# Storing a transform's first rows ahead of the rest, and a maximum negated per sign: one change to a fused FFT and gated MLP kernel

## The chip, the cores and the metric

One core of one Trainium2 chip. The metric is device time in microseconds (us) for one launch. The kernels were timed in rounds beside runs of the kernel before on the same chip. Single runs of one kernel differ (the kernel before: 1200.54 to 1205.46), so parts of a few us are read from the trace, and totals from several rounds.

The traces name the engines of the core: PE multiplies matrices, DVE does vector work, ACT functions and copies, POOL small sums and some transfers, SP issues most transfers. SBUF is the memory on the chip, DRAM the one beside it.

## The reference

```python
X = np.fft.fft(np.fft.fft(x, axis=1), axis=2).real      # x: (8, 3136, 256)
h = X.reshape(25088, 256) @ w_in                        # d_ff = 1024
e = np.exp(h - h.max(-1)); sm = e / (e.sum(-1) + 1e-9)
u = h * sm
ln = (u - mean(u)) / sqrt(var(u) + 1e-6) * g_ln
out = ln @ w_out                                        # back to 256
```

The weights come as 64-bit floats and are converted on the chip by integer operations.

## The kernel before

The sequence of 3136 is split as 49 x 64. Two batches form a pair. For each pair a first transform of length 49 runs in eight pieces c, called quarters in these texts (`transform1`, 98 rows in, 100 rows out: 25 frequencies k1 with 4 parts j each). Its result z goes to DRAM (`zd`), and comes back turned (`turn`: 5 frequencies at a time) for the second transform. Then 25 units per pair follow, one for each k1: up-products, maximum, exponential, product, square, transposition, and, four units later, the down-product. A unit has two signs (k1 and its mirror), but k1 = 0 has one. For pairs 1 to 3 the transform runs beside the units of the pair before. For pair 0 nothing hides it: this start is what the change is about.

```python
def transform1(pr, s):                       # cut
    c, l = divmod(2 * s, CH)
    if l == 0:
        if pr.p == 0 and c % 2:              # two buffers z_u and two buffers z
            z = fpool.tile([P, FF], FP32, tag="u", name="z_u", bufs=2)
            pr.z = z[0:ZR].rearrange("p (l d) -> p l d", l=CH)
        else:
            pr.z = zpool.tile([ZR, CH, D], FP32, tag="z", name="z")
    ...                                      # matmuls into ps
    nc.scalar.copy(pr.z[:, l : l + 2, :], ps[0:ZR])
    if l == CH - 2:
        nc.sync.dma_start(out=pr.zd[:, c * CH : (c + 1) * CH, :], in_=pr.z)   # ZR = 100 rows

def turn(pr, i):
    pr.g[i] = gpool.tile([P, KG, D], FP32, tag="g", name="g")                 # six buffers
    for j in range(4):
        k = j * NK + i * KG
        nc.gpsimd.dma_start(out=pr.g[i][j * NH : (j + 1) * NH, :, :],
                            in_=pr.zd[k : k + KG, :, :].rearrange("k n d -> n k d"))

# join(): both maxima, then one negation of both; expo(): exponential of each sign
nc.scalar.mul(out=t.neg[:, 0:n], in_=t.nmax[:, 0:n], mul=-1.0)

# the start
for c in range(NC):                          # cut
    add_mirror(first, c, nc.vector); fold(first, c)
    ...                                      # c == 3: load raw_out, the output weights
    for s in range(CH // 2): transform1(first, c * CH // 2 + s)
turn(first, 0)
...
for i in range(KF * D // NW): weights.narrow_out(i)      # DVE converts raw_out to Wo: 4 times
for t in units[:2]: take2(t, transform2(pairs[0], t.k1)); spread(t)           # spread loads r
# unit: even() = L223 needs r, Wi, w_mid; unit 0 also centres Wo (L457 to L459)
```

Of the kernel before, what the change touches and what calls it, by code (L numbers as in the profile page):

```python
# [9 lines left out]
FP32 = mybir.dt.float32  # L10
# [6 lines left out]
P = 128  # L17


N1, N2 = 49, 64  # L20
NK = N1 // 2 + 1
# [3 lines left out]
CH = 4  # L25
# [9 lines left out]
def kernel(  # L35
# [57 lines left out]
    class Pair:  # L93
        def __init__(self, p):
            self.p = p
            self.raw, self.y, self.y0 = {}, {}, None
            self.g = {}

    def load(pr, c, room=None):

# [42 lines left out]
    def transform1(pr, s):  # L143



        c, l = divmod(2 * s, CH)
        if s == 0:
            pr.zd = dram.tile([ZR, NH, D], FP32, tag="zd", name="zd")
        if l == 0:  # L150
            if pr.p == 0 and c % 2:

                z = fpool.tile([P, FF], FP32, tag="u", name="z_u", bufs=2)
                pr.z = z[0:ZR].rearrange("p (l d) -> p l d", l=CH)
            else:
                pr.z = zpool.tile([ZR, CH, D], FP32, tag="z", name="z")
        y = pr.y[c]
        ps = ps_m.tile([P, 2, D], FP32, tag="m", name="ps1")
        if s == NH // 2 - 1:
            parts = [(ps[0:ZR, 0], y[:, l], 0), (ps[0:ZR, 1], pr.y0[:, 0], 1), (ps[0:ZR, 1], y[:, l + 1], 2)]  # L160
        else:
            parts = [(ps[0:ZR], y[:, l : l + 2], 0)]
        first = True
        for o, i, t in parts:
            for h, cs in enumerate((EVEN, ODD)):
                nc.tensor.matmul(o[..., cs], F[:, 2 * t + h, :], i[..., cs], start=first, stop=True,  # L166
                                 skip_group_check=True)
                first = False
        nc.scalar.copy(pr.z[:, l : l + 2, :], ps[0:ZR])
        if l == CH - 2:  # L170
            nc.sync.dma_start(out=pr.zd[:, c * CH : (c + 1) * CH, :], in_=pr.z)

    def turn(pr, i):

        pr.g[i] = gpool.tile([P, KG, D], FP32, tag="g", name="g")
        for j in range(4):
            k = j * NK + i * KG
            nc.gpsimd.dma_start(out=pr.g[i][j * NH : (j + 1) * NH, :, :],  # L178
                                in_=pr.zd[k : k + KG, :, :].rearrange("k n d -> n k d"))

    def transform2(pr, k1):

# [43 lines left out]
    def join(t, ps):  # L226

        t.nmax = small.tile([P, 2], FP32, tag="nmax", name="nmax")
        for s in t.signs:
            t.h[s] = fpool.tile([P, FF], FP32, tag="h", name="h", bufs=2)  # L230
            nc.vector.tensor_tensor_reduce(out=t.h[s], in0=t.ev, in1=ps, scale=1.0, scalar=-3.0e38,  # L231
                                           op0=ALU.subtract if s else ALU.add, op1=ALU.max,
                                           accum_out=t.nmax[:, s : s + 1])
        n = len(t.signs)
        t.neg = small.tile([P, 2], FP32, tag="neg", name="neg")
        nc.scalar.mul(out=t.neg[:, 0:n], in_=t.nmax[:, 0:n], mul=-1.0)  # L236

    def expo(t):
        t.esum = small.tile([P, 2], FP32, tag="esum", name="esum")
        for s in t.signs:  # L240
            t.u[s] = fpool.tile([P, FF], FP32, tag="u", name="u", bufs=2)
            nc.scalar.activation(out=t.u[s], in_=t.h[s], func=ACT.Exp, bias=t.neg[:, s : s + 1],  # L242
                                 accum_out=t.esum[:, s : s + 1])
# [71 lines left out]
    def down(t, s):  # L315
        uT = t.batch.uT[:, t.w].rearrange("p c i (n s) -> p c (i n) s", s=2)
        ps = ps_m.tile([P, D], FP32, tag="m", name="ps_o")
        for c in range(KF):
            nc.tensor.matmul(ps, uT[:, c, :, s], Wo[:, c, :], start=(c == 0), stop=(c == KF - 1))  # L319
        return ps  # L320

    def scale(t, s, ps):
        t.ot[s] = fpool.tile([P, D], FP32, tag="ot", name="ot", bufs=6)
        nc.scalar.mul(out=t.ot[s], in_=ps, mul=t.rs[:, s : s + 1])  # L324
# [165 lines left out]
    with tc.manual_schedule():  # L490
# [25 lines left out]
        for c in range(NC):  # L516
# [16 lines left out]
                transform1(first, c * CH // 2 + s)  # L533
            if c == 3:
                weights.product_in(0)
        turn(first, 0)
        weights.place_table()
        for h in range(1, 3):
            weights.product_in(h)
# [9 lines left out]
        for i in range(len(units) + lag):  # L549
            cur = units[i] if i < len(units) else None  # L550
            nxt = units[i + 2] if i + 2 < len(units) else None
            old = units[i - lag] if i >= lag else None
            ahd = pairs[cur.p + 1] if cur and cur.p + 1 < NP else None
            last = i >= len(units) - 2
            prv = units[i - 1] if 0 < i <= whole else None
            if i > lag:
                store(units[i - lag - 1])
            if cur:
                if i % 2 == 0:
                    batch = Batch(i >= whole)  # L560
                cur.batch, cur.w = batch, i % 2
                even(cur, up(cur, 0))
                odd = up(cur, 1)
            if nxt:
                take2(nxt, transform2(pairs[nxt.p], nxt.k1))
                spread(nxt)
            if prv:
                turn_whole(prv)
            if cur:
                join(cur, odd)  # L570
            if prv:
                for o, ps in prv.wait:
                    nc.vector.tensor_copy(out=o, in_=ps)
            if cur:
                expo(cur)
            if ahd:
                ahead_pe(ahd, cur.k1)
            if old:
                ps_o = [down(old, s) for s in old.signs]
            if cur:  # L580
                for s in cur.signs:
                    product(cur, s)
                if i == 0:
                    weights.centre()
                for s in cur.signs:
                    square(cur, s)
                    if i >= whole:
                        turn_blocks(cur, s)
            if old:
                scale(old, 0, ps_o[0])  # L590
            if cur:
                if last:
                    move_blocks(batch, slice(cur.w, cur.w + 1), (nc.sync, nc.gpsimd) if cur.w else (nc.sync,))
                elif cur.w and i >= whole:
                    move_blocks(batch, slice(0, 2))
                stats(cur)
            if 0 < i + 1 < NK // KG:
                turn(first, i + 1)
            if ahd:
                ahead(ahd, cur.k1)  # L600
            if old and 1 in old.signs:
                scale(old, 1, ps_o[1])
        store(units[-1])


def _tables(B, S, D):

    import numpy as np

    def cs(num, den):  # L610
        a = 2.0 * math.pi * (num % den) / den
        return np.cos(a), np.sin(a)

    n1, k1 = np.arange(N1)[:, None], np.arange(NK)[None, :]
    c, s = cs(n1 * k1, N1)
    cm, sm = cs((n1 - N1 // 2) * k1, N1)
    zero = np.zeros_like(c)
    tabs = [(c, s), (s, -c), (c, zero), (s, zero), (zero, cm), (zero, sm)]
    f = np.zeros((2, N1, 6, 2, 2, NK))
    for t, (u, v) in enumerate(tabs):  # L620
        for b in range(2):
            f[b, :, t, b, 0], f[b, :, t, b, 1] = u, v
    k = (np.arange(NK)[:, None] + N1 * np.arange(N2)[None, :])[None]
    n2 = (np.arange(NH) + 1) % NH
    c, s = cs(n2[:, None, None] * k, S)
    t = np.stack([c, -s])
    t[1, -1] = 1.0 - 2.0 * (k[0] % 2)
    m, d = np.arange(D)[:, None], np.arange(D)[None, :]
    q = np.where(d <= D // 2, cs(m * d, D)[0], -cs(m * (d - D // 2), D)[1])

    q = np.concatenate([q, q[:, D // 2 : D // 2 + 1]], axis=1)
    q[:, D // 2] = 0.0
    sign = np.where(np.arange(P) == 0, 1.0, -1.0)[:, None]
    row = np.arange(B)[:, None] * N1 + np.arange(N1)[::-1]

    load = row.reshape(-1, PR, 1) * (N2 // CH) + N2 // CH - 1 - np.arange(NC)
    mirror = np.zeros((P, B // 2 * (NC + NK - 1)), np.int32)
    mirror[:PR, : B // 2 * NC] = load.transpose(1, 0, 2).reshape(PR, -1)
    rows = np.arange(B)[:, None, None] * S + (N1 - np.arange(1, NK)) + N1 * np.arange(N2)[::-1, None]
    mirror[:, B // 2 * NC :] = rows.reshape(B // 2, P, NK - 1).transpose(1, 0, 2).reshape(P, -1)  # L640
    return {
        "f_tab": f.reshape(PR, 6, ZR).astype(np.float32),
        "t_tab": t.reshape(2 * NH, NK, N2).astype(np.float32),
        "q_tab": q.astype(np.float32),
        "sign": sign.astype(np.float32),
        "mirror": mirror,
    }
# [32 lines left out]
```

## Time and profile before

| | before |
|---|---|
| time, median of the first 3 runs | 1204.17 us (1202.84 to 1204.25) |
| profiled span, mean granted clock | 1200.8 us, 0.993 |
| busy: PE, DVE, ACT, POOL | 96%, 75%, 53%, 45% |
| second transform of unit 0 starts | 68.25 us |
| first vector step of unit 0 (L223) | 73.04 us |
| first down-product (L319) | 107.65 us |
| last scaling on ACT, end of the span | 1196.01, 1200.8 us |

PE is the engine in short supply from 110 us on, so time can be won only before that or after its last product. In the page's part 2 the span is cut into 40 slices of 30 us; a digit is the busy share in tenths. Of the kernel before:

```profile
PE   2868999999999999999999999999999999999998
DVE  8778877777768877777767887877777787777770
```

Only the first four digits of PE and the last are low, and in the first four DVE is busy there. The prediction shows these slices in detail.

### The profile page before, as it was taken

To read this page: it belongs to the slowest core of one execution; us is meant where nothing else is said; L and a number is where in the kernel's file an instruction comes from. 1 tells how busy PE (TensorE), PEld (TensorE's weight loads), DVE (VectorE), ACT (ScalarE), POOL (GpSimd) and SP (SyncE) were. 2 spreads that over 40 slices of the span, in tenths; PEclk is the share of its full clock that TensorE was granted. 3 is DMA by queue.
4 is the path that set the end of the run, shared out by engine and by line. 5 is a ranking of instruction groups with operands and counts; after the bars stand their busy time and mean duration, and the time that the engine had idled before them with its cause. 6 is when DMAs were issued, how large, how long until landed. Compare 5 with 4: busy or idle time off the path is not lost. (4 is left out here: it accounts for less than half of the span.)

```text
span 1200.8 us, 15804 instructions
## 1 busy us (share of the span) xinstructions
PE 1155.5 (96%) x4720; PEld 877.0 (73%) x4720; DVE 905.8 (75%) x1255; ACT 640.4 (53%) x1286; POOL 543.8 (45%) x966
## 2 busy tenths in 40 slices
PE   2868999999999999999999999999999999999998
PEld 1446777777777777777777777777877777777787
DVE  8778877777768877777767887877777787777770
ACT  1337555655555655655554665655554555555551
POOL 3046545554645555443554555444453333333333
PEclk9989999999999999999999999999999999999999
DMA  9833799978999798777999799797899586776765
GB/s 237 257 92 82 142 174 162 192 134 158 184 162 170 167 177 164 175 132 140 169 178 189 144 185 166 159 168 137 160 171 159 94 139 115 134 129 109 132 111 114
DMA packets 457382, 184.98 MB, mean 154 GB/s; under 512 B 425510, under 2 KB 439086, under 8 KB 457296
## 3 DMA queue, kind: packets, MB, share of 16 engines
q1 hardware_dynamic: 443216, 144.89, 68.5%
q0 software_dynamic: 14080, 39.08, 12.4%
q8 instruction: 38, 0.62, 0.2%
q14 instruction: 48, 0.39, 0.1%
HBM read 44.37 MB, written 38.80 MB: 69 GB/s over the span
## 5 line engine op out<-in xcount | busy, mean ns | idle before, releaser
L319 PE MATMUL ps_o<-Wo,uT 128*128 128x256 f32 x3136 | 693.4, 379 | 0.0
L319 PEld LDWEIGHTS ps_o<-Wo,uT 128*128 128x128 f32 x3136 | 611.6, 196 | 61.8 <-issue 1.0
L217 PE MATMUL ps_h<-Wi,q 128*128 128x512 f32 x800 | 362.5, 596 | 0.1
L250 DVE SCALAR_TENSOR_TENSOR u<-h,u 128x1024 f32<-128x1024 f32 x196 | 232.6, 1223 | 153.5 <-ACT u L242 95.7
L259 ACT ACTIVATE h<-u,nmean 128x1024 f32<-128x1024 f32 x196 | 223.7, 1142 | 123.4 <-POOL nmean L252 123.3
L252 POOL TENSOR_SCALAR nmean<-usum 128x1 f32<-128x1 f32 x196 | 127.0, 649 | 348.4 <-DVE u L250 348.1
L231 DVE CUSTOM_DVE_ANT_0 h<-ev,ps_h 128x1024 f32<-128x1024 f32 x196 | 231.8, 1219 | 44.6 <-PE ps_h L217 38.4
L217 PEld LDWEIGHTS ps_h<-Wi,q 128*128 128x128 f32 x800 | 152.7, 191 | 150.0 <-issue 143.9
L287 DVE STREAM_TRANSPOSE v<-u 128x1024 f32<-128x1024 f32 x192 | 228.2, 1230 | 0.1
L242 ACT ACTIVATE u<-h,neg 128x1024 f32<-128x1024 f32 x196 | 223.6, 1142 | 3.3
L223 DVE SCALAR_TENSOR_TENSOR ev<-w_mid,r,ps_h 128x1024 f32<-128x1024 f32 x100 | 127.7, 1277 | 55.0 <-PE ps_h L217 49.8
L195 ACT COPY q<-ps 128x256 f32<-128x256 f32 x100 | 37.2, 372 | 183.0 <-PE ps L189 155.5
L331 POOL DMA_INDIRECT out_dram<-ot,idx x96 | 102.8, 1071 | 33.3 <-issue 18.4
L236 ACT ACTIVATE neg<-nmax 128x2 f32<-128x2 f32 (+1 forms) x100 | 20.4, 204 | 175.2 <-DVE nmax L231 140.8
L189 PEld LDWEIGHTS ps<-T,g 128*128 128x128 f32 x400 | 60.9, 194 | 59.0 <-issue 56.8
L271 POOL TENSOR_SCALAR v<-ssq 128x2 f32<-128x2 f32 (+1 forms) x100 | 27.6, 276 | 167.2 <-ACT h L259 167.2
L166 PE MATMUL ps<-y,F 98*100 98x258 f32 (+3 forms) x288 | 72.7, 390 | 24.6 <-DVE y L122 23.8
L324 ACT ACTIVATE ot<-ps_o,rs 128x256 f32<-128x256 f32 x196 | 83.3, 459 | 24.0 <-DMA out_dram<-ot,idx 12.8
L274 POOL TENSOR_TENSOR rs<-v,neg_half 128x2 f32<-128x2 f32 (+1 forms) x100 | 72.5, 725 | 7.8
L166 PEld LDWEIGHTS ps<-y,F 98*100 98x100 f32 x288 | 46.3, 179 | 37.0 <-DVE y L122 21.3
L189 PE MATMUL ps<-T,g 128*128 128x128 f32 x400 | 61.6, 278 | 11.3 <-DMA g<-zd 11.3
L178 POOL DMA_DIRECT2D g<-zd x80 | 47.8, 607 | 47.2 <-DMA zd<-z_u 38.7
(68 smaller groups left out, 465.0 us busy)
## 6 DMA issues: line engine op xcount, KB each, us to landing
uT<-v SPq DMA_DIRECT2D x752, 128.0 KB
g<-zd POOLq DMA_DIRECT2D x80, 160.0 KB, 4.8
out_dram<-ot SPq DMA_DIRECT2D x100, 128.0 KB
zd<-z SPq DMA_DIRECT2D x28, 400.0 KB
xa<-in_x_dram SPq DMA_DIRECT2D x28, 392.0 KB
raw_in<-in_moe_w_in_dram SPq DMA_DIRECT2D x4, 512.0 KB
raw_out<-in_moe_w_out_dram SPq DMA_DIRECT2D x2, 1024.0 KB
zd<-z_u SPq DMA_DIRECT2D x4, 400.0 KB
```

The lines of the kernel that those rows point to most:

```text
L166: nc.tensor.matmul(o[..., cs], F[:, 2 * t + h, :], i[..., cs], start=first, stop=True, skip_group_check=True)
L189: nc.tensor.matmul(ps[:, h * P : (h + 1) * P], g[:, k, h * P : (h + 1) * P], T[:, k1, :], start=(h == 0), stop=True, skip_group_check=True)
L217: nc.tensor.matmul(ps[:, fs], t.q[:, c * P : (c + 1) * P], Wi[:, c, fs], start=True, stop=True)
L223: nc.vector.scalar_tensor_tensor(out=t.ev, in0=w_mid, scalar=t.r, in1=ps, op0=ALU.mult, op1=ALU.add)
L231: nc.vector.tensor_tensor_reduce(out=t.h[s], in0=t.ev, in1=ps, scale=1.0, scalar=-3.0e38, op0=ALU.subtract if s else ALU.add, op1=ALU.max, ...
L242: nc.scalar.activation(out=t.u[s], in_=t.h[s], func=ACT.Exp, bias=t.neg[:, s : s + 1], accum_out=t.esum[:, s : s + 1])
L250: nc.vector.scalar_tensor_tensor(out=t.u[s], in0=t.h[s], scalar=1.0, in1=t.u[s], op0=ALU.mult, op1=ALU.mult, accum_out=t.usum[:, s : s + 1])
L252: nc.gpsimd.tensor_scalar(out=t.nmean[:, s : s + 1], in0=t.usum[:, s : s + 1], scalar1=-1.0 / FF, scalar2=None, op0=ALU.mult)
L259: nc.scalar.activation(out=t.h[s], in_=t.u[s], func=ACT.Square, bias=t.nmean[:, s : s + 1], accum_out=t.ssq[:, s : s + 1])
L287: nc.vector.transpose(out=t.batch.v[:, t.w, :, o], in_=t.u[s])
L319: nc.tensor.matmul(ps, uT[:, c, :, s], Wo[:, c, :], start=(c == 0), stop=(c == KF - 1))
L331: dma = nc.gpsimd.indirect_dma_start(out=out, out_offset=bass.IndirectOffsetOnAxis(ap=idx[:, i : i + 1], axis=0), in_=t.ot[s], in_offset=None)
```

## The change

The intent: the second transform needs, for its first five frequencies, only 20 of the 100 rows of each quarter. So rows are laid out frequency first, 20 rows of each quarter are stored at once, the first turn is issued on two queues, and only then do the other 80 rows follow, from buffers kept for it (four of the six g buffers, which are free at that time). Beside it, the maxima are negated by sign, and the last unit's two signs swap places so that the last store is a direct one (the other sign's rows are stored indirectly, through a table of row numbers).

```diff
-            if pr.p == 0 and c % 2:
+            if pr.p or c < 2:
+                pr.z = zpool.tile([ZR, CH, D], FP32, tag="z", name="z")
+            elif c < 4:
                 z = fpool.tile([P, FF], FP32, tag="u", name="z_u", bufs=2)
                 pr.z = z[0:ZR].rearrange("p (l d) -> p l d", l=CH)
             else:
-                pr.z = zpool.tile([ZR, CH, D], FP32, tag="z", name="z")
+                pr.z = gpool.tile([P, KG, D], FP32, tag="g", name="z_g")[0:ZR, 0:CH, :]
+            pr.zs[c] = pr.z
@@
-            nc.sync.dma_start(out=pr.zd[:, c * CH : (c + 1) * CH, :], in_=pr.z)
+            keep(pr, c, slice(0, ZR if pr.p else 4 * KG))
+    def keep(pr, c, rows):
+        nc.sync.dma_start(out=pr.zd[rows, c * CH : (c + 1) * CH, :], in_=pr.zs[c][rows])
@@ turn: rows as (k j), engines[j] in place of nc.gpsimd
@@
-        t.neg = small.tile([P, 2], FP32, tag="neg", name="neg")
-        nc.scalar.mul(out=t.neg[:, 0:n], in_=t.nmax[:, 0:n], mul=-1.0)
@@ expo, in its loop over the signs
+            nc.scalar.mul(out=t.neg[:, s : s + 1], in_=t.nmax[:, s : s + 1], mul=-1.0)
@@
-        turn(first, 0)
+        turn(first, 0, (nc.sync, nc.gpsimd) * 2)
+        for c in (2, 3, 0, 1, 4, 5, 6, 7):
+            keep(first, c, slice(4 * KG, ZR))
@@
-                ps_o = [down(old, s) for s in old.signs]
+                order = old.signs[::-1] if old is units[-1] else old.signs
+                ps_o = [down(old, s) for s in order]
@@ scale() and the table of the first transform follow the new orders
```

## The prediction

> **What bounds the kernel now.** The page gives PE 96% of the span at a granted clock of 0.993, so I asked where the other 4% lies. The table of busy time by stretch (columns: stretch, its length, busy us with instruction counts of PE, PEld, DVE, ACT, POOL, then PE clock, DMA share, GB/s) answers:
>
> ```profile
> core 0: us, PE busy (x) PEld busy (x) DVE busy (x) ACT busy (x) POOL busy (x), PEclk, DMA share, GB/s
> 40.00:50.00 10.00, 9.21 (x45) 6.42 (x44) 6.45 (x16) 4.24 (x7) 0.00 (x0) 1.00 0.93 276
> 50.00:60.00 10.00, 6.95 (x17) 2.77 (x15) 8.45 (x18) 3.79 (x4) 0.00 (x0) 1.00 0.64 245
> 60.00:70.00 10.00, 1.75 (x8) 1.78 (x9) 9.04 (x19) 2.52 (x4) 2.48 (x4) 0.59 0.28 82
> 70.00:80.00 10.00, 10.00 (x34) 6.28 (x33) 4.72 (x6) 3.48 (x7) 1.11 (x2) 0.90 0.26 67
> 110.00:120.00 10.00, 10.00 (x42) 7.53 (x41) 8.28 (x12) 5.78 (x12) 5.92 (x10) 1.00 0.27 68
> ```
>
> From about 110 us PE is 10.00 of 10 in every stretch up to 1190. There each unit costs PE about 11 us of matmuls, and nothing in this stage leaves PE waiting. So any time won must be won before 110 us, or after PE's last matmul. A hole stands at 57 to 68 us, PE nearly idle. The table of waits for the first 70 us (waiter, awaited, us in total, times, longest) names it:
>
> ```profile
> POOL g L178 <- DMA zd<-z_u: 38.7, 1, 38.7
> PE ps L189 <- DMA g<-zd: 11.3, 1, 11.3
> ACT z_u L169 <- DMA zd<-z_u: 9.6, 2, 6.6
> DVE tmp L357 <- DMA raw_out<-in_moe_w_out_dram: 3.5, 1, 3.5
> ```
>
> The second transform (L189) waits for the turned buffer g, this for the last store of the first transform, this for its copy on ACT, and that one for an earlier store of the same buffer z_u. The timeline (start, us, engine, what, count) shows the same chain and, beside it, DVE:
>
> ```profile
> 47.41 0.16 DVE L122 COPY y<-x 98x2 f32<-98x2 f32 x1
> 51.10 0.43 DVE L357 TENSOR_SCALAR tmp<-raw_out 128x512 int32<-128x512 int32 x1 [3.53 <-DMA raw_out<-in_moe_w_out_dram]
> 56.20 1.07 ACT L169 COPY z_u<-ps 100x512 f32<-100x512 f32 x2 [6.57 <-DMA zd<-z_u]
> 57.29 0.27 SPq L171 DMA_DIRECT2D zd<-z_u  x1
> 63.02 2.48 POOL L178 DMA_DIRECT2D g<-zd  x4 [38.74 <-DMA zd<-z_u]
> 68.25 2.05 PE L189 MATMUL ps<-T,g 128*128 128x128 f32 x8 [11.30 <-DMA g<-zd]
> 68.64 0.88 DVE L380 SCALAR_TENSOR_TENSOR Wo<-raw_out,g_ln,tmp 128x256 f32<-128x256 f32 x2
> ...
> 73.04 1.28 DVE L223 SCALAR_TENSOR_TENSOR ev<-w_mid,r,ps_h 128x1024 f32<-128x1024 f32 x1 [3.52 <-PE ps_h L217]
> ...
> 79.02 2.29 DVE L459 TENSOR_TENSOR Wo<-Wo,wbar 128x2048 f32<-128x2048 f32 x1 [0.31 <-ACT wbar L458]
> ...
> 81.23 1.27 DVE L223 SCALAR_TENSOR_TENSOR ev<-w_mid,r,ps_h 128x1024 f32<-128x1024 f32 x1
> ...
> 85.29 1.15 ACT L242 ACTIVATE u<-h,neg 128x1024 f32<-128x1024 f32 x1
> ```
>
> The point to see is that two chains end together. PE starts at 68.25, but DVE converts the output weights (L357 to L380) from 51.10 to 69.52 and then waits only 3.52 us for PE. A first turn ten us earlier cannot be worth ten us unless DVE also finishes sooner.
>
> **What the Trainium skill says.** "DMA: Bandwidth & Descriptors", section "Why a DMA increments its semaphore by 16 and not by 1", says that a hardware-queue transfer runs on the largest number of engines, up to 16, that divides the slowest dimension of both sides, and names 100 partitions as 10. The trace agrees: while only stores of 100 rows are left (50 to 60 us) the DMA share is 0.64, near 10 of 16. By it the new 20-row stores have 10 engines, the 80-row ones 16.
> The same page, "Queues, rings and completion order", says that each engine consumes one queue's descriptors in ring order and alternates between queues by packets. So a tiny later load on SP's queue waits behind earlier stores; no number before shows that alone, and the change makes it matter. "Anatomy of one DMA" puts the fixed cost near 2.0 us for the software path; the lone first load here (idx, hardware queue) was issued at 0.74 and released POOL at 2.94, 2.2 us.
> "TensorE: Matmul & The Clock Gate", Part 1, says that the clock halves after an idle window of about 3.4 us and needs about as long to return. Agrees: last matmul 56.95, clock 0.50 from 62, work again at 68.25, clock 0.97 in 72 to 73.
>
> **The change, part by part.**
> (1) Bytes. Eight stores of 400 KB before the first turn become eight of 80 KB; 8 x 320 KB = 2.6 MB move behind it. Of this, stores 1 to 3 (28.72 to 35.78) lie ahead of the weight load raw_out (issued 38.33) in SP's queue: 0.98 MB less on 10 engines at 245 GB/s, 4 us. raw_out lands near 47 instead of 51. DVE's folds end at 47.57, before and after (they wait only 1.43 and 1.10 us, for things the change does not touch). So DVE starts converting at 47.6, not 51.1, and ends at 47.6 + 18.4 = 66.0, not 69.5: **3.5 us**.
> (2) Buffers. The last four quarters take g buffers, so ACT no longer waits 6.57 us. PE ends the first transform at 50.1; copies end near 50.7; the last store is issued near 50.8 instead of 57.29 and, with the queue almost empty, lands about 2.5 us later: 53.5. The turn is issued from two queues, 1.2 us instead of 2.48, and lands 2.7 us after its end (68.2 less 65.5 before): 57.5 to 58.5. PE is then free (product ends at 56.95). The second transform starts near **58, ten us earlier**; both halves of the first unit's up-product are ready by 63.
> (3) The late stores. 2.6 MB and part of the turn's 0.66 MB go ahead of the load of r, which L223 also needs. At 330 to 390 GB/s (the table shows 331 and 387 where all 16 engines work) 3.3 MB take 8 to 10 us from 54.5: drained at 63 to 64.5, r lands near 65 to 66. That is about when DVE comes free, so I count no cost but see the largest risk here.
> (4) So L223 for unit 0 starts at about 66.0 instead of 73.04: **7.0 us**, 3.5 from DVE and 3.5 from its wait for PE.
> (5) The column-sum product of the weights (16 matmul records, 3.6 us before) must wait for DVE's 66.0. PE will have idled 3 us or more, so probably part of it runs at half clock: ready at 70 (warm) to 71.5. L459 then starts at 71.4 to 72.3 against 79.02, a gain of 7.6 to 6.7; I take **6.7**, thus minus 0.3 on (4).
> (6) Negation by sign: 96 more ACT instructions of 204 ns, 20 us spread over ACT's 53%: hidden. In unit 1 the exponential of the first sign needs no longer wait for the second maximum: nmax at 83.87, ACT's copies done at 84.07, exponential at 85.29; it could start at 84.3: **1.0 us**. In units 2 to 4 the loop is exponential, product, mean, square, copies to uT, negation: 7.69 us a unit (88.86, 96.55, 104.24). ACT is still copying to uT until 92.73 when both maxima are nearly there (92.70), so nothing more is won.
> (7) The end. The last unit's sign order is reversed, so its last store is a direct one.
>
> ```profile
> 1196.01 0.47 ACT L324 ACTIVATE ot<-ps_o,rs 128x256 f32<-128x256 f32 x1 [2.98 <-PE ps_o L319]
> 1196.76 0.97 POOL L331 DMA_INDIRECT out_dram<-ot,idx  x1 [5.43 <-ACT ot L324]
> ```
>
> Now the indirect store takes 4.0 us from 1196.76 to the span's end at 1200.8. The direct one could be issued at 1196.5 and lands some 2.5 us later, 1199.0; the indirect one then starts 3.4 us earlier and ends first: **1.7 us**.
> (8) The interleaved row order changes addresses, not packets (1 KB) or bytes: 0.
> Sum: 6.7 + 1.0 + 1.7 = 9.4 us. I take 0.4 off for r or raw_out coming a little late: 9.0, hence 1195.2 us.
>
> **The rivals.**
> A: r comes late, the wait for g replaced by a wait for r. For it: the ring order and SP's long issue times under load (15.62 us once). If the late stores drain at 250 GB/s, 13 us from 54.5, r lands near 69: 4 us gained at (4), about 1199. Against: 80 rows spread over 16 engines.
> B: DVE does not move, because raw_out still waits for earlier x loads. Then only the 3.5 us wait for PE goes: total near 6, 1198. For it: DMA share is 0.93 to 1.00 up to 50 us.
> C: PE stays bound and the extra ACT work or the late stores' traffic slow the steady stage, so nothing is gained: 1204. Against: PE there has no waits for ACT worth naming and the late stores end before 70.
> D: better than thought: clock stays up and r is early: 8.6 + 1.7, 1193.5; with folds shortened too, 1191.
>
> **Range and chances.** Centre 1195.2, A and B give the upper side, D the lower: 1191 to 1199.5. Two per cent is 24 us, more than the whole hole before 68 us could give, since DVE's chain holds: faster 0.02, same 0.97, slower 0.01.
>
> **What will show it.** Right: first L189 near 58; first conversion of raw_out near 47.6 without a wait; first L223 near 66 with neither PE nor r as a long releaser; unit 1's exponential about 7.7 us earlier; PE full from about 100 us; the chain that ended last is a direct store. Wrong: L223 idle on r, conversion still waiting on raw_out, or a longer mean of the down-product L319 (379 ns) in the steady stage.

## The result

The changed kernel takes 1195.16 us (median of 6 runs, 1194.22 to 1200.61), the kernel before 1203.78 (6 runs): 8.6 us less. The ratio is 0.9938, 95% interval 0.9916 to 0.9960; a ratio is the mean time of one kernel's runs over that of the other's of the same rounds, so not quite the ratio of the medians. A second series (e11 below) gave 1195.89 against 1203.71, ratio 0.9939.

The lines of the changed kernel that answer to those in the prediction. First the waits of the first 70 us (lines have moved: L357 is L361, L223 is L228, L189 is L194):

```profile
POOL g L184 <- DMA zd<-z_g: 28.7, 1, 28.7
PE ps L194 <- DMA g<-zd: 3.7, 1, 3.7
DVE ev L228 <- DMA r<-q: 0.5, 1, 0.5
```

The wait of ACT for a z buffer (9.6 us) and that of DVE for raw_out (3.5 us) are gone, PE's wait for g fell from 11.3 to 3.7 us, and a new wait of 0.5 us for r has come. The timeline:

```profile
47.72 0.42 DVE L361 TENSOR_SCALAR tmp<-raw_out 128x512 int32<-128x512 int32 x1
52.91 0.80 SPq L184 DMA_DIRECT2D g<-zd  x2
60.42 1.13 PE L194 MATMUL ps<-T,g 128*128 128x128 f32 x8 [3.67 <-DMA g<-zd]
62.62 5.70 SPq L205 DMA_DIRECT2D r<-q  x3
65.40 0.88 DVE L384 SCALAR_TENSOR_TENSOR Wo<-raw_out,g_ln,tmp 128x256 f32<-128x256 f32 x2
66.76 1.28 DVE L228 SCALAR_TENSOR_TENSOR ev<-w_mid,r,ps_h 128x1024 f32<-128x1024 f32 x1 [0.48 <-DMA r<-q]
72.12 2.29 DVE L463 TENSOR_TENSOR Wo<-Wo,wbar 128x2048 f32<-128x2048 f32 x1
```

and at the end:

```profile
1189.31 0.47 ACT L328 ACTIVATE ot<-ps_o,rs 128x256 f32<-128x256 f32 x1 [2.98 <-PE ps_o L323]
1189.81 0.33 SPq L339 DMA_DIRECT2D out_dram<-ot  x1
```

The late stores follow the turn on SP's queue from 53.77 on. PE's second transform starts 7.8 us earlier, but DVE's first step of unit 0 only 6.3 us earlier (73.04 to 66.76), because DVE converts weights until 66.28.

To follow the time through, I cut the span of each profiled run at the same four events. The three columns before the last are stages: from the first vector step to the first down-product, from there to the last scaling, from there to the end.

| run | raw_out conversion starts | 2nd transform | unit 0 on DVE | to first down | steady | tail | span |
|---|---|---|---|---|---|---|---|
| before | 51.10 | 68.25 | 73.04 | 34.61 | 1088.36 | 4.8 | 1200.8 |
| changed | 47.72 | 60.42 | 66.76 | 34.06 | 1088.49 | 3.6 | 1192.9 |
| difference | -3.38 | -7.83 | -6.28 | -0.55 | +0.13 | -1.2 | -7.9 |
| e1 early only | 46.65 | 59.32 | 65.59 | 35.27 | 1088.94 | 4.8 | 1194.6 |
| e2 negation, order | 50.84 | 68.63 | 73.89 | 33.37 | 1090.55 | 3.2 | 1201.0 |
| e3 split at once | 49.07 | 62.29 | 67.42 | 33.85 | 1088.94 | 3.6 | 1193.8 |
| e4 late stores after r | 47.20 | 57.40 | 65.65 | 33.99 | 1089.06 | 3.5 | 1192.2 |
| e5 conversion cut | 48.81 | 61.63 | 68.16 | 34.87 | 1088.99 | 3.6 | 1195.6 |
| e6 cut, late after r | 46.93 | 57.00 | 60.23 | 36.63 | 1088.57 | 3.6 | 1189.0 |
| e7 96 + 4 rows | 48.51 | 62.91 | 68.47 | 34.91 | 1088.32 | 4.8 | 1196.5 |
| e8 loads later | 47.00 | 57.17 | 65.53 | 34.36 | 1089.43 | 3.6 | 1192.9 |
| e9 loads earlier | 46.54 | 57.22 | 65.08 | 32.19 | 1088.78 | 3.5 | 1189.6 |
| e10 and one part deferred | 48.69 | 57.97 | 62.46 | 35.25 | 1088.99 | 3.5 | 1190.2 |
| e11 changed again | 46.38 | 58.76 | 65.46 | 34.04 | 1088.58 | 3.5 | 1191.6 |

The nine runs that store 20 rows first (changed, e1, e4 to e6, e8 to e11) are alike up to the conversion, yet start it anywhere from 46.38 to 48.81: the start of a run jitters by 2.4 us. Single traces are therefore compared by the length of a stage, not by its clock time, where less than that matters.

### The profile page after: what moved, and what is told of

Read it like the earlier page. It is cut to its first block, busy times and chain, and to the rows that moved or that the text cites. A ratio compares the mean times of both kernels' runs of the same rounds, so it can differ in the third digit from the quotient of the medians.

```text
span 1192.9 us, 15912 instructions
## 1 busy us (share of the span) xinstructions
PE 1154.9 (97%) x4720; PEld 876.3 (73%) x4720; DVE 915.5 (77%) x1255; ACT 666.2 (56%) x1382; POOL 494.4 (41%) x964
## 4 chain that ended last, share of the span: by engine, by line
PE 92%; ACT 1%; issue 1%; DVE 0%; POOL 0%; ACTq 0%; DVEq 0%
PE ps_o L323 57%; PE ps_h L222 28%; PE ps L169 4%; PE ps L194 4%; ACT u L246 0%; ACT h L263 0%; POOL nmean L256 0%; DVE h L236 0%; PE ps_t L303 0%; DVE u L254 0%; ACT uT L308 0%; ACT q L200 0%; DVE uT L579 0%; ACT ot L328 0%; ACT neg L244 0%
## 5 line engine op out<-in xcount | busy, mean ns | idle before, releaser
L254 DVE SCALAR_TENSOR_TENSOR u<-h,u 128x1024 f32<-128x1024 f32 x196 | 240.1, 1226 | 56.8 <-ACT u L246 30.3
L256 POOL TENSOR_SCALAR nmean<-usum 128x1 f32<-128x1 f32 x196 | 81.2, 415 | 448.0 <-DVE u L254 447.9
L228 DVE SCALAR_TENSOR_TENSOR ev<-w_mid,r,ps_h 128x1024 f32<-128x1024 f32 x100 | 127.8, 1278 | 131.7 <-PE ps_h L222 125.4
L328 ACT ACTIVATE ot<-ps_o,rs 128x256 f32<-128x256 f32 x196 | 86.8, 462 | 61.1 <-PE ps_o L323 55.0
L194 PEld LDWEIGHTS ps<-T,g 128*128 128x128 f32 x400 | 60.1, 191 | 51.3 <-issue 50.1
L278 POOL TENSOR_TENSOR rs<-v,neg_half 128x2 f32<-128x2 f32 (+1 forms) x100 | 82.7, 827 | 7.8
L244 ACT ACTIVATE neg<-nmax 128x1 f32<-128x1 f32 x196 | 38.3, 195 | 62.5 <-DVE nmax L236 61.5
L275 POOL TENSOR_SCALAR v<-ssq 128x2 f32<-128x2 f32 (+1 forms) x100 | 23.2, 232 | 114.4 <-ACT h L263 114.4
L194 PE MATMUL ps<-T,g 128*128 128x128 f32 x400 | 60.7, 275 | 3.7 <-DMA g<-zd 3.7
```

What stands on the lines that cost most here:

```text
L194: nc.tensor.matmul(ps[:, h * P : (h + 1) * P], g[:, k, h * P : (h + 1) * P], T[:, k1, :], start=(h == 0), stop=True, skip_group_check=True)
L228: nc.vector.scalar_tensor_tensor(out=t.ev, in0=w_mid, scalar=t.r, in1=ps, op0=ALU.mult, op1=ALU.add)
L254: nc.vector.scalar_tensor_tensor(out=t.u[s], in0=t.h[s], scalar=1.0, in1=t.u[s], op0=ALU.mult, op1=ALU.mult, accum_out=t.usum[:, s : s + 1])
L328: nc.scalar.mul(out=t.ot[s], in_=ps, mul=t.rs[:, s : s + 1])
```

## The experiments

Theory after the first look: the gain is 6.3 us at the start, set by DVE's conversion and not by the ten us of PE; 1.2 us at the end; something small from the negation. Rivals: the bytes taken out of the queue do it; the buffers do it; the loads of g or r set the start.

**e1: only the early start.** The negation of both signs at once and the old order are put back.

```diff
-            nc.scalar.mul(out=t.neg[:, s : s + 1], in_=t.nmax[:, s : s + 1], mul=-1.0)
+        nc.scalar.mul(out=t.neg[:, 0:n], in_=t.nmax[:, 0:n], mul=-1.0)     # ahead of the loop
-                order = old.signs[::-1] if old is units[-1] else old.signs
+                order = old.signs
```

> The early first turn with its buffers and late stores, but the negation of both signs at once and the old order of the last unit. Theory (time comes from the moved start, 6.5 us, and from the end, 1.2 us; the negation by sign gives nothing): the first L223-like instruction stays near 66.8 us, PE's last matmul near 1189 us as in the changed kernel, the span ends 4.8 us after the start of the last scaling instead of 3.6: 6 to 7 us under the kernel before. Rival (the negation by sign gives its 1.0 us): 5.5 us under it, and unit 5 starts 1 us later than in the changed kernel.

Measured: 1197.45 us against 1203.34, 5.9 us less, ratio 0.9953 (0.9939 to 0.9966). The tail is 4.8 us again. But the stage up to the first down-product is 35.27 us instead of 34.06: the negation by sign is worth 1.2 us, so on that point the rival was right. (Over all runs whose work in this stage is otherwise nearly the same: 34.61 to 35.27 us in three runs without it, 33.37 to 34.06 in five with it.)

**e2: only the negation and the order**, on the kernel before (the edit is the reverse).

> The kernel before with only the negation by sign and the reversed order at the end. Theory: the exponential of unit 1 starts 1 us earlier relative to its first vector step, but POOL is then busy with the first turn of later rows and two indirect loads, so the means come no earlier and unit 5 starts when it did; only the end gains, 1.2 us. Total 1.0 to 1.5 us under before. Rival: 2.2 us under before, with unit 5 one us earlier.

Measured: 1202.12 against 1203.34, ratio 0.9994 (0.9981 to 1.0008), not separable from no change; in total the theory was nearer than the rival. The trace tells why. The stage up to the first down-product is 33.37 against 34.61 us, again 1.2 us less, and the tail 3.2 against 4.8. But in this run the steady stage is 2.2 us longer: PE came to its first down-products after pauses, and the granted clock was 0.50 from 108 to 110 us and 0.77 from 110 to 112. So my theory that the negation gains nothing is refuted by the stages of e1 and e2 alike, though e2's total did not keep the gain.

Where it gains, in us after unit 0's first vector step:

| | before | e2 | e1 | changed |
|---|---|---|---|---|
| exponential of unit 1 | 12.25 | 11.14 | 11.63 | 10.48 |
| squares of unit 1 | 16.02 | 15.13 | 16.68 | 15.82 |
| squares of unit 2 | 23.71 | 21.80 | 24.37 | 22.49 |
| squares of unit 3 | 31.40 | 30.14 | 32.05 | 30.84 |
| first down-product | 34.61 | 33.37 | 35.27 | 34.06 |

With the negation by sign (e2 against before, changed against e1) 1.1 us are there at unit 1's exponential, as predicted, and 0.9 remain at its squares. Unit 2's squares add 1.0, and unit 3's lose 0.7 of it (ACT waits there 1.72 us for the mean in the changed kernel, 1.40 in e1).

What unit 2 adds was not foreseen. The views are timelines of e1 (first) and of the changed kernel (second): POOL's means of the product, and the square on ACT that waits for the first of them.

```profile
88.79 1.34 POOL L257 TENSOR_SCALAR nmean<-usum 128x1 f32<-128x1 f32 x2 [0.27 <-DVE u L255]
89.96 1.15 ACT L264 ACTIVATE h<-u,nmean 128x1024 f32<-128x1024 f32 x1 [1.40 <-POOL nmean L257]
```

```profile
88.98 0.23 POOL L256 TENSOR_SCALAR nmean<-usum 128x1 f32<-128x1 f32 x1 [0.15 <-DVE u L254]
89.25 1.15 ACT L263 ACTIVATE h<-u,nmean 128x1024 f32<-128x1024 f32 x1 [0.26 <-POOL nmean L256]
```

In e1 DVE's second product (two SBUF operands, 1.22 us) begins as POOL is about to do its one-column mean, and the mean is through only when that product is about done: ACT waits 1.40 us. With the negation in two steps the second exponential, and so the second product, comes 0.2 us later; POOL's mean slips in between, takes 0.23 us, and ACT waits 0.26 us. The Trainium skill, "SBUF — State Buffer", sections "SBUF: two separate sides" and "Who interferes with whom", says that a DVE instruction with two SBUF inputs contends with a GpSimd instruction that reads SBUF, and that whichever starts first holds the shared ports for its whole length. The traces agree. Of the 196 means, 93 took over 0.6 us in the kernel before and 35 in the changed one (the others at most 0.38 us). Each of these long ones began while a DVE instruction with two SBUF inputs was running (a product, once the centring L463) and ended 0.09 to 0.1 us after it. Over the whole run ACT's waits for the mean were 123.3 us before and 124.8 in e1, but 65.8 in e2 and 66.0 in the changed kernel. In the steady stage this wins nothing (1088.94 us in e1, 1088.49 in the changed kernel), as PE is the bound there.

**e3: the 80 rows right behind the 20.** The g buffers stay; the same bytes as before the change lie ahead of raw_out and of the turn.

```diff
             keep(pr, c, slice(0, ZR if pr.p else 4 * KG))
+            if pr.p == 0:
+                keep(pr, c, slice(4 * KG, ZR))
@@
-        for c in (2, 3, 0, 1, 4, 5, 6, 7):
-            keep(first, c, slice(4 * KG, ZR))
```

> The changed kernel, but each quarter's other 80 rows are stored right behind its first 20 instead of after the first turn; the extra g buffers stay. Theory (half the gain of the start comes from bytes taken from ahead of raw_out): conversion of raw_out again waits about 3 us and starts near 50.5 to 51, L228 of unit 0 near 69.5 to 70, total 3 us over the changed kernel, the second transform starting near 63. Rival (only the buffer wait mattered): conversion still starts at 47.7, L228 near 66.8, total as the changed kernel.

Measured: 1195.77 against 1203.34, ratio 0.9936, as good as the changed kernel: the rival's total, though with neither's clock times.

```profile
49.07 0.43 DVE L363 TENSOR_SCALAR tmp<-raw_out 128x512 int32<-128x512 int32 x1 [1.41 <-DMA raw_out<-in_moe_w_out_dram]
62.29 2.05 PE L196 MATMUL ps<-T,g 128*128 128x128 f32 x8 [5.68 <-DMA g<-zd]
```

The second transform does come 1.9 us later than in the changed kernel, but DVE waits only 1.41 us for raw_out instead of 3.53 (before) and 4.40 (e2). With bytes deferred the nine runs show waits of 0 to 1.29 us. So the deferral of 2.6 MB, the heart of the change, accounts for about 1 us of DVE's earlier start (1.41 us less the nine runs' mean of 0.39; e3 is one trace). Something else that e3 shares with the changed kernel gives the rest: the form of the stores, or the buffers.

**e7: the form of the stores alone.** On the kernel before, with its buffers, its order and its late turn, each store of 100 rows becomes one of 96 and one of 4.

```diff
-            nc.sync.dma_start(out=pr.zd[:, c * CH : (c + 1) * CH, :], in_=pr.z)
+            for rows in (slice(0, 96), slice(96, ZR)) if pr.p == 0 else (slice(0, ZR),):
+                nc.sync.dma_start(out=pr.zd[rows, c * CH : (c + 1) * CH, :], in_=pr.z[rows])
```

> The kernel before, with each store of 100 rows of the first pair split into one of 96 and one of 4 rows, same bytes at the same place in the order. Theory (100 rows run on 10 engines, 96 on 16, so raw_out no longer waits for ten crowded engines): DVE waits 1 to 2 us for raw_out instead of 3.5 to 4.4, the first turn and the second transform come 1.5 to 3 us earlier, total 2 us under before. Rival (only the bytes count): unchanged within 0.7 us.

Measured: 1197.72 against 1203.66, 5.9 us less, ratio 0.9950 (0.9936 to 0.9963), three times what was expected. By the medians it equals e1, with neither its early turn nor its buffers nor its deferral. (The single traces lie further apart: e7's profiled run, one of its slower ones, has a span 4.3 us under before, e1's, its fastest, 6.2.) From the timeline:

```profile
48.51 0.43 DVE L358 TENSOR_SCALAR tmp<-raw_out 128x512 int32<-128x512 int32 x1 [1.97 <-DMA raw_out<-in_moe_w_out_dram]
62.91 2.05 PE L190 MATMUL ps<-T,g 128*128 128x128 f32 x8 [7.43 <-DMA g<-zd]
68.47 1.28 DVE L224 SCALAR_TENSOR_TENSOR ev<-w_mid,r,ps_h 128x1024 f32<-128x1024 f32 x1 [1.47 <-PE ps_h L218]
```

And a row of the table by stretch, of the kernel before and of e7 (its last two columns are DMA share, the mean busy share of the core's 16 DMA engines, and GB/s):

```profile
50.00:52.00 2.00, 2.00 (x6) 0.87 (x5) 0.85 (x2) 0.00 (x0) 0.00 (x0) 1.00 0.69 254
```

```profile
50.00:52.00 2.00, 2.00 (x6) 0.87 (x5) 1.93 (x4) 0.00 (x0) 0.00 (x0) 1.00 1.05 404
```

The share is 1.05 at 404 GB/s, where the kernel before had 0.69 and 254. What held the engines is seen in the single DMA packets that the traces hold; raw_out's are the only ones of 2 KB on SP's queue up to 80 us. (Busy time of packets for each us gives the number of engines at work, a few per cent too high; the trace doesn't name the engines.) In the kernel before, from 44 to 46 us, packets of 4 KB, of which the stores consist, hold 9 to 10 engines and raw_out's only 6. From 48 to 51 us nothing but raw_out is under way, on ten engines: six have done their share of it, ten were kept behind by the stores of 100 rows. In e7 raw_out moves on all 16 from 45 to 49 us. From its first packet to its last it took 14.5 us before and 15.3 in e2, 8.6 in e7, 9.0 in e3 and 8.8 to 10.7 in the nine runs that store 20 rows first. The prediction used the rule for the rate of the stores (10 engines) and for the new ones, but not for what the same bytes would do on 16. ACT's wait for z_u stays here (5.8 us), so the buffers were not needed for this gain.

**e4: the late stores behind r.** In the changed kernel the 80-row stores are issued after the first two loads of r.

```diff
         for t in units[:2]:
             take2(t, transform2(pairs[0], t.k1))
             spread(t)
+        for c in (2, 3, 0, 1, 4, 5, 6, 7):
+            keep(first, c, slice(4 * KG, ZR))
```

> The changed kernel with the late stores put behind the first two loads of r on the queue. Theory (late stores delay g and r, but DVE's conversion ends at 66.3 anyway): second transform near 57.5 instead of 60.4, r lands near 61.5, L228 of unit 0 at 66.3 with no wait: 0.5 us or less gained in total. Rival (g and r are what sets the start): L228 and the total 3 us earlier.

Measured: 1194.09 against 1203.34, ratio 0.9929 (0.9915 to 0.9942); the theory held.

```profile
57.40 1.13 PE L194 MATMUL ps<-T,g 128*128 128x128 f32 x8 [1.54 <-DMA g<-zd]
65.65 1.27 DVE L228 SCALAR_TENSOR_TENSOR ev<-w_mid,r,ps_h 128x1024 f32<-128x1024 f32 x1
```

The late stores had held up g by about 3 us, and the second transform now starts 3.0 us earlier; unit 0 starts without a wait, but still only when the conversion is done. By the medians the gain over the changed kernel is about 1 us, but the intervals overlap.

**e5 and e6: the conversion cut** (wrong result: two of the four conversions run only their last two instructions). e5 on the changed kernel, e6 on e4.

```diff
+        if cut:                                  # parts 2 and 3
+            for i, (o, scale) in enumerate(outs):
+                r = slice(i * n, (i + 1) * n)
+                nc.vector.scalar_tensor_tensor(out=o, in0=unit[:, r].bitcast(FP32), scalar=scale,
+                                               in1=unit[:, r].bitcast(FP32), op0=ALU.mult, op1=ALU.mult)
+            return
```

> The changed kernel with two of the four conversions of raw_out cut to their last two instructions (wrong result on purpose): DVE is through about 7 us sooner, near 59. Theory (the load of r, held up by the late stores, stands right behind the conversion as a second wall at 66.7): L228 of unit 0 now waits about 6 us for r and starts at 66 to 67, total as the changed kernel within 1 us. Rival (the conversion alone sets the start): L228 near 61 to 62, total 4 to 5 us lower.

> The same cut, together with the late stores behind the first two loads of r (wrong result on purpose). Theory: with both walls gone the start is set by PE and r at 61 to 62: total 4 to 5 us under the changed kernel. If a further wall stands behind, less.

Measured: e5 1196.17, ratio 0.9936, no faster than the changed kernel; e6 1190.70, ratio 0.9892 (0.9877 to 0.9907), both against 1203.66. One line from each:

```profile
68.16 1.28 DVE L228 SCALAR_TENSOR_TENSOR ev<-w_mid,r,ps_h 128x1024 f32<-128x1024 f32 x1 [8.45 <-DMA r<-q]
```

```profile
60.23 1.28 DVE L228 SCALAR_TENSOR_TENSOR ev<-w_mid,r,ps_h 128x1024 f32<-128x1024 f32 x1 [2.50 <-PE ps_h L222]
```

In the changed kernel two walls stand side by side. Taking away DVE's (e5) turns 0.5 us of wait for r into 8.45; taking away r's (e4) leaves DVE's; with both gone (e6) unit 0 starts 6.5 us sooner and waits for PE. Only 4.0 us of these reach the first down-product (96.86 against 100.82), as the stage up to it grew to 36.63 us: the next turn on POOL waited 2.18 us and ACT 3.81 us for unit 1's means behind it. The profile puts the turn's wait down to r; the turn doesn't read r, but it does read the rows of the late stores ahead of r in the same queue, so I take it to be these (not shown).

**e8 and e9: POOL's queue.** In the changed kernel unit 1's exponential starts 8.0 us earlier than before, its squares only 6.5 (82.58 against 89.06; in e1 8.1 and 6.8, so this comes with the early start): the means stand in POOL's queue behind a turn and two indirect loads for pair 1. e8 (on e4) issues the two loads two units later, e9 before unit 0.

```diff
-        if step == 0:
+        if step == (2 if pr.p == 1 else 0):      # e8
+        if step == 0 and pr.p > 1:               # e9, with load(pairs[1], 0) and (.., 1) before the units
```

> The version with the late stores behind r, and the second pair's first two indirect loads issued two units later, so that POOL is free for the means of unit 1. Theory (the means of unit 1 stood 2 us in POOL's queue behind a turn and two loads): squares of unit 1 start about 2.4 us earlier after L228 of unit 0, the first down-product about 1.5 us earlier, total 1 to 1.5 us under the version without it. Rival (ACT's loop sets the pace anyway): unchanged.

> The late stores behind the first two loads of r, and the second pair's first two loads issued before unit 0 instead of two units later (which only moved the 2.3 us in POOL's queue from unit 1's means to unit 3's). Theory (POOL's queue holds up the means of whatever unit the two loads stand in): no unit's squares wait over 1.8 us, first down-product near 97.6 instead of 99.6 us, total 1.5 to 2 us under the version with the loads in unit 1. Rival (ACT's loop makes up for it): within 0.7 us of that version.

Measured: e8 1195.15 against 1203.66 (0.9935), no better than e4, so in total the rival held. Unit 1's squares did come 2.6 us sooner (78.87 against 81.43 in e4), but the same hold-up came back in unit 3:

```profile
94.99 0.96 POOL L109 DMA_INDIRECT xb<-in_x_dram,idx  x1 [0.30 <-issue]
96.31 1.15 ACT L263 ACTIVATE h<-u,nmean 128x1024 f32<-128x1024 f32 x1 [2.70 <-POOL nmean L256]
```

e9 puts the loads where POOL has nothing else: 1193.20 against 1203.71, ratio 0.9919 (0.9905 to 0.9932), the stage to the first down-product 32.19 us, 1.8 under e4. From unit 1 on no squares wait over 1.74 us, so the theory held in the trace; the timed gain over e4, about 1 us where 1.5 to 2 were expected, is within the intervals.

**e10: part of the conversion deferred** (on e9, a correct kernel). The last of the four conversions goes behind unit 0's exponential, the centring into unit 1.

```diff
-        for i in range(KF * D // NW):
+        for i in range(KF * D // NW - 1):
@@ in the loop over units
                 expo(cur)
+                if i == 0:
+                    weights.narrow_out(KF * D // NW - 1)
@@
-                if i == 0:
+                if i == 1:
                     weights.centre()
```

> The same, and the last of the four conversions of raw_out put behind unit 0's exponential, with the centring of the weights in unit 1. Theory (the conversion is the last wall before unit 0, and some of it fits into DVE's waits for ACT): L228 of unit 0 near 61.5, total 1 to 3 us under the version without it. Rival (DVE's work is only moved to where DVE is as full): within 0.7 us.

> The changed kernel once more, on the same chip as the two above, for a comparison of like with like: 8 to 9 us under before, as in its first runs.

Measured on one chip against 1203.71: e10 1190.90, ratio 0.9894 (0.9878 to 0.9909); e11, the changed kernel, 1195.89, ratio 0.9939 (0.9925 to 0.9952). So e10 beats both kernels, by 12.8 and 5.0 us. Over e9 the medians say 2.3 us, but the intervals overlap a little. From the start of the conversion to the first down-product e10 took 49.02 us (48.69 to 97.71), e9 50.73 (46.54 to 97.27), so 1.7 us of it shows in the trace; the size remains uncertain.

## Why the prediction was right, and which of its steps were not

Time and direction were right: 1195.2 forecast, 1195.16 measured. Part of this closeness is luck, since errors cancel; step by step:

- **(1) raw_out earlier, conversion from 47.6 to 66.0.** The times were right (47.72 to 66.28, a gain of 3.4 against 3.5 us), with some luck: the nine runs start it between 46.38 and 48.81. The cause was half right. I put it to 0.98 MB fewer bytes on ten engines ahead of raw_out. Ten engines did hold it up, but the bytes need not go: e3 has all of them ahead of raw_out and DVE still waits only 1.41 us, and spreading the stores over 16 engines alone (e7) leaves 1.97 of 3.53 to 4.40. The deferral adds about 1 us.
- **(2) Second transform near 58.** 60.42; the copies and the store came as said, and the turn was issued from 52.91 to 54.83. The step that failed is the landing "2.7 us after its end": with the late stores alongside it took 5.6 us from POOL's last issue (54.83) to PE's start. In e4, without them, it took 3.1 us (54.26 to 57.40).
- **(3) r lands at 65 to 66.** It cost 0.48 us. It was rightly called the largest risk: e5 shows it as a second wall.
- **(4), (5)** Unit 0 on DVE 6.3 us earlier (7.0 said), the centring L463 6.9 us earlier (6.7 said).
- **(6) Negation, 1.0 us from unit 1, nothing in units 2 to 4.** Right in size and place for unit 1: 1.1 us at its exponential in both pairs of runs, 0.9 at its squares. "Nothing more" failed: unit 2 won 1.0 by means no longer blocked behind DVE's second product, and unit 3 lost 0.7, so that 1.2 us reached the first down-product.
- **(7) The end, 1.7 us.** 1.2: from the last scaling to the end 4.8 us with the indirect store last (three runs), 3.2 to 3.6 with the direct one (ten runs).
- **Sum.** 9.4 said and 9.0 taken; 7.9 in the two profiled runs (6.28 + 0.55 - 0.13 + 1.2), 8.6 and 7.8 in the medians of two series. The over-sized terms are (4) by 0.7 and (7) by 0.5. Up to unit 1's exponential the 7.7 us said (6.7 and 1.0) were there, 8.0; POOL's queue took 1.5 of them before its squares.
- **Rivals.** B (DVE doesn't move) and C (steady stage pays) are refuted: the steady stage is 1088.36 and 1088.49 us. Only A showed a trace of itself: r was late, by 0.48 us. D, at 1193.5, did not come. Two of their sums are wrong: A's r at 69 gives 4 + 1.0 + 1.7 us, so 1197.5 and not 1199, and D's 8.6 + 1.7 gives 1193.9.

What stays open: how the remaining 0 to 1.29 us of wait for raw_out come about, and how much of the jitter of the start, 2.4 us, is due to the DMA queues.

## What to carry to other kernels

When a wait on one engine is removed, look first for what stands beside it: here DVE's conversion and the load of r ended within 0.5 us of each other, and PE's eight us were worth six. Check the row count of every large transfer: by the medians 100 rows instead of 96 + 4 cost this kernel 5.9 us, as much as the whole restructured start gained (e1). A small operation on an engine with a queue full of DMA issues, or beside a two-operand DVE instruction, may wait longer than it works; moving the issue elsewhere helps only if that place is idle.

## What the Trainium skill lacked or had wrong

- "DMA: Bandwidth & Descriptors", section "Why a DMA increments its semaphore by 16 and not by 1": its rule for the number of engines agrees with every run (share 0.63 for 100 rows, up to 1.05 once split), but beyond a remark elsewhere on the page that a bulk load runs at the pace of its slowest engine, it doesn't say what an uneven load does to the transfers behind it: DVE's wait for a 16-engine load behind 100-row stores was 3.5 to 4.4 us, with 96 + 4 rows 2.0 us.
- The same page gives no figure for a small load behind large stores in one queue: r, 0.5 KB, came some 4 us after its issue (62.62 to 66.7), and in e6, with the stores behind it, in at most 2.1 us (58.12 to 60.23).
- "TensorE: Matmul & The Clock Gate", Part 1, speaks of an idle window of about 3.4 us (and, in its second failure mode, of short pauses without a length). Here a pause of 2.1 us, in the kernel before, was also followed by the half clock, but not every such pause is: e2 had one of 2.0 us up to 91.71, and its clock stayed 1.00 until 96. The kernel before (its timeline, then a row of its table by stretch, third column from the end the clock):

```profile
91.74 0.65 PE L299 MATMUL ps_t<-ident,u 128*128 128x128 f32 x4 [2.09 <-ACT q L195]
```

```profile
93.00:94.00 1.00, 1.00 (x2) 0.46 (x2) 0.91 (x2) 1.00 (x1) 0.99 (x2) 0.50 0.04 0
```

- No page that I read compares the end of an indirect store with that of a direct one: the last scaling to the end took 4.8 and 3.2 to 3.6 us.
